# Block 1 of a long convolution goes forward by tokens modulo 4, and GpSimd multiplies gate by up where both lie in SBUF as bf16

## The chip, the cores and the metric

The kernel runs on one core of one Trainium2 chip. The metric is the device time of one execution in microseconds (us), the median of three runs: 909.69 us before the change (909.67 to 910.05). The profile is one more execution, recorded by the hardware profiler. Its engines are TensorE (PE; PEld is its weight load), VectorE (DVE), ScalarE (ACT), GpSimd (POOL) and SyncE (SP, which only issues DMAs).

## The reference, cut to what matters

Four layers follow each other: gated convolution (A), feed-forward (B), A, B, each on a layernorm of x and added to x. S is 2048 tokens, D 576 channels, F 4608.

```python
def A(q, k, v, shift_k, ssm_k, ssm_D):
    k_shift = sum over t of k_pad[:, t:t+S, :] * shift_k[:, ks-1-t]      # four taps
    kv = k_shift * v
    y = causal convolution of kv with ssm_k along the tokens (by FFT), as bf16
    return q * (y + kv * ssm_D)
def B(x, w_gate, w_up, w_down):
    return (gelu(x @ w_gate) * (x @ w_up)) @ w_down
x = x + A(layernorm(x)); x = x + B(layernorm(x)); x = x + A(layernorm(x)); x = x + B(layernorm(x))
```

The convolution's k, v and filter are the same in both A layers, so y is computed once and used twice.

## The kernel before, in words

**Feed-forward.** The tokens are cut into four chunks of 512. A unit is one chunk in one B layer; there are eight units. A unit's 36 tiles of F (128 wide) are done in three parts of 12, and the program goes through 24 *visits* (0 to 23), each one part of one unit. Visits 0 to 2 are unit 0 (chunk 0, first B layer), visits 3, 5 and 7 unit 1 (chunk 1), visits 4, 6 and 8 unit 2, visits 9, 11 and 13 unit 3, visits 10, 12 and 14 unit 4, and so on. For each tile, `gu` (L1103) makes gate and up side by side in one of three PSUM banks that go round; then the tile goes one of two ways (L1689 to L1704). Either ScalarE makes gelu(gate) as fp32 and VectorE multiplies it by up straight from PSUM (L1700, L1701); or ScalarE writes both gelu(gate) and up into SBUF as bf16 (L1691, L1692), so that the bank is free without VectorE, and VectorE multiplies the two there (L1693). The second way is taken while convolution work waits for VectorE. The pair in SBUF is a tile `ga` out of a ring of two; the products are `hT`. After twelve tiles the down part (`two_rows`, L1752, matmuls at L1768) multiplies hT by w_down for the four rows of 128 tokens; a tile's product may be needed from the first matmuls of the down part on.

**Convolution.** It is done by transforms of 512 tokens per block, four blocks. Block 0 is done in a prologue ahead of visit 0. Blocks 1 to 3 are worked off beside the feed-forward matmuls: VectorE makes kv (`kv_ops`, L255 to L267); TensorE transforms the filter's block and kv's block forward in 16 steps; ScalarE evicts each step's result from PSUM to an fp32 tile `eo` (two of its own ring, two of the ring `yh`); VectorE adds and subtracts the halves of eo (`cross`, L333); VectorE multiplies the spectra and sums them (`prod`, L341 to L345, L552), combines them (L353, L358) and folds them (L587, L588); TensorE transforms back (L373 in block 1, L310 in blocks 2 and 3) and ScalarE or VectorE writes y (L697, L700). y of block c is needed before the units of chunk c.

**Forward steps.** For block 1 (`fwd`, `fwd_h`, `fwd_eo`, L469, L497, L295) a step takes one half of the frequencies modulo 2, sums over all four token residues i = 0 to 3 and needs 8 matmuls of 64x288; eo holds the even and the odd tokens' sums, and one `cross` of two VectorE instructions (128x288) finishes two spectra. For blocks 2 and 3 (`fwd4`, `quarter`, L620, L321) a step takes only two token residues (e and e+2) and needs 4 matmuls; a first `cross` makes sums and differences in fp32 tiles `ab` and `cd` (ring `ac`), and for every second step four more VectorE instructions (L656) combine them.

```python
295     def fwd_eo(self, src, kt, s, h, ring, scale=1.0):
...
299                                    [([self.fw(kt, s, i + e) for e in range(2)],
300                                      [src(i + e)[:, h * HW:(h + 1) * HW] for e in range(2)]) for i in (0, 2)])
...
321     def quarter(self, src, e, s, h, scale=1.0):
...
325         ps = yield from self.both_steps(lambda ps: [ps[:, n, 0:HW] for n in range(2)],
326                                    [([self.fw(0, s, i) for i in ij], [src(i)[:, h * HW:(h + 1) * HW] for i in ij])])
```

**What sets the order.** While the program is built, a planner keeps a clock for each engine (`Pace`, L46: `t.pe`, `t.dve`, `t.act`) from cost constants (L29 to L43) and decides where each convolution instruction is put among the feed-forward's. VectorE's convolution work is the list `V`, its adds after forward steps the list `U`, TensorE's steps the list `Pq`, GpSimd's loads the list `L`; `fill` (L1168) drains them after each tile and in the down part. On the chip every engine goes through its instructions in the order so fixed, and waits on semaphores. GpSimd before the change issues DMAs (spectra out to and back from DRAM, L377, L443, L448, L457; k, v, x; outputs L381) and works on statistics of one element per partition (L933, L948, L949). Statistics are put into its order up to AHEAD = 2.0 us before the planner expects their input (L935, L951).

Of the kernel before, what the change touches and what calls it, by code (L numbers as in the profile page):

```python
# [17 lines left out]
P = 128  # L18
# [17 lines left out]
C_HB = 0.345  # L36
C_FOLD = 0.46
C_TURN, DRAIN = 0.0, 0.35
LAG = 0.25
AHEAD = 2.0  # L40
# [5 lines left out]
class Pace:  # L46


    def __init__(self):
        self.pe = self.dve = self.act = 0.0  # L50
# [84 lines left out]
class Conv:  # L135
# [159 lines left out]
    def fwd_eo(self, src, kt, s, h, ring, scale=1.0):  # L295

        nc = self.nc
        ps = yield from self.both_steps(lambda ps: [ps[:, e, 0:HW] for e in range(2)],
                                   [([self.fw(kt, s, i + e) for e in range(2)],
                                     [src(i + e)[:, h * HW:(h + 1) * HW] for e in range(2)]) for i in (0, 2)])  # L300
        eo = self.eo_tile(ring)
        nc.scalar.activation(out=eo[:], in_=ps[:, :, 0:HW], func=ACT.Copy, scale=scale)
        return eo

# [89 lines left out]
    def step(self, m, kv=None, loaded=False):  # L394
# [74 lines left out]
        def fwd(kt, s, h):  # L469
            def run():  # L470
                if s == 0 and h == 0:
                    for k in (kt, kt + 2):
                        kc[k] = self.kcp.tile([P, 2, D], BF16, tag="kc", name="kc")
                free, ring = self.eo_free(True)
                self.eo_at[ring].popleft()
                cur = self.cur
                eo = yield from self.fwd_eo(lambda i: self.vt_[m][:, i, :], kt, s, h, ring)
                done = t.on_act(C_EVA, max(t.pe + 0.25 + LAG, free))
                self.ps_free[cur] = done
                if (kt, s, h) == (1, 1, 1):  # L480
                    self.fwd_at[m] = t.pe + 0.25
                cols = slice(h * HW, (h + 1) * HW)

                def fin():
                    self.cross(eo, kc[kt][:, s, cols], kc[kt + 2][:, s, cols])
                    when = t.on_dve(2 * C_BF, done + LAG)
                    self.eo_at[ring].append(when + LAG)
                    mark(("kc", kt, s, h), when + LAG)
                    if s == 1 and h == 1 and m < self.NB - 1:
                        for k in (kt, kt + 2):  # L490
                            self.spill(self.Kd[m][k], kc[k], when + LAG)
                self.U.append((done + LAG, 2 * C_BF, fin))
            return run

        hh = self.hh if m == 1 else {}

        def fwd_h(kt, s, h):  # L497
            def run():
                if (kt, s, h) == (0, 0, 0):
                    self.hh_tiles()  # L500
                free, ring = self.eo_free(True)
                self.eo_at[ring].popleft()
                cur = self.cur
                eo = yield from self.fwd_eo(self.ht[m], kt, s, h, ring, 1.0 / NFQ)
                done = t.on_act(C_EVA, max(t.pe + 0.25 + LAG, free))
                self.ps_free[cur] = done
                if (kt, s, h) == (1, 1, 1):
                    self.hf_at[m] = t.pe + 0.25
                    if loaded:
                        self.hr_free[0] = self.hr_free[1] = self.hf_at[m]  # L510
                cols = slice(h * HW, (h + 1) * HW)

                def fin():
                    self.cross(eo, hh[kt][:, s, cols], hh[kt + 2][:, s, cols])
                    when = t.on_dve(2 * C_BF, done + LAG)
                    self.eo_at[ring].append(when + LAG)
                    mark(("hh", kt, s, h), when + LAG)
                    if s == 1 and h == 1:
                        for k in (kt, kt + 2):
                            self.spill(self.Hd[m][k], hh[k], when + LAG)  # L520
                        if kt == 1:
                            self.hd_at[m] = when + 10.0
                self.U.append((done + LAG, 2 * C_BF, fin))
            return run
# [95 lines left out]
        def fwd4(filt, e, s, h):  # L620
# [3 lines left out]
            def run():  # L624
                free = self.eo_at["eo"].popleft()
                cur = self.cur
                eo = yield from self.quarter(src, e, s, h, scale)
                done = t.on_act(C_EVA, max(t.pe + 0.13 + LAG, free))
                self.ps_free[cur] = done
                if last:  # L630
                    (self.hf_at if filt else self.fwd_at)[m] = t.pe + 0.13
                cols = slice(h * HW, (h + 1) * HW)

                def first():
# [4 lines left out]
                    else:  # L639
                        if s == 0 and h == 0:  # L640
# [4 lines left out]
                    self.eo_at["eo"].append(t.on_dve(2 * C_BF, done + LAG) + LAG)  # L645

                def second(n):
                    def run():
# [9 lines left out]
                        if n == 1 and last:  # L658
# [7 lines left out]
                            if filt:  # L666
                                self.hd_at[m] = when + 10.0
                    return run
# [40 lines left out]
    def run_loads(self):  # L709
        t = self.t  # L710
        self.flush(t.pe)
        while self.L and self.L[0][0]() <= t.pe - 0.3:
            self.L.popleft()[1]()

# [73 lines left out]
def ssm_geglu_kernel(ctx, tc, A_q, A_k, A_v, A_shift_k, A_ssm_k, A_ssm_D, B_x, B_w_gate, B_w_up,  # L788
# [137 lines left out]
    def mean_after(v, when):  # L926
# [8 lines left out]
        conv.spills.append((when - AHEAD, run))  # L935

    def square_task(get_x, v):
        def run():
# [12 lines left out]
            conv.spills.append((when - AHEAD, root))  # L951
# [255 lines left out]
    with tc.manual_schedule():  # L1207
# [432 lines left out]
        for at, (wb, ph, ui, first, final) in enumerate(visits):  # L1640
# [34 lines left out]
            for fi in range(FP):  # L1675
# [13 lines left out]
                if (hurry() or conv.V and not aq) and t.act <= t.pe + 0.2:  # L1689
# [3 lines left out]
                    nc.vector.tensor_tensor(out=hT[:, fi, :], in0=ga[:, 0, :], in1=ga[:, 1, :], op=ALU.mult)  # L1693
                    there = t.on_act(2 * C_GELU, max(t.pe + 0.15, gone[0]))
                    gone.append(t.on_dve(C_HB, there + 0.15) + 0.1)
# [174 lines left out]
```

## Time and profile before

| what | value |
|---|---|
| median of three runs (range) | 909.69 us (909.67 to 910.05) |
| profiled execution: span from first to last instruction | 907.9 us |
| PE busy | 902.9 us (99%) |
| DVE busy | 556.8 us (61%) |
| ACT busy | 364.5 us (40%) |
| POOL busy | 142.0 us (16%) |
| first gate/up tile of visit 0 | at 44.7 us of the span |
| down part of visit 0 begins | 66.4 us |
| visit 1 begins | 83.05 us |
| visit 2 begins | 118.1 us |
| visit 3 begins | 157.1 us |

The profiled execution's span is what the recorder saw; the runs' time is 1.8 us longer, which lies around the span. A row of a group of instructions reads: line, engine, operation, output tile <- input tiles, partitions x elements, count | busy us, mean ns of one | idle time of the engine ahead of them and what ended it. A row of stages reads: stretch in us from the span's start, its length, then for each engine the busy us and the number of instructions. A row of a source line reads: count, shortest/median/longest in ns. A row of the timeline reads: start, length, instruction, count of merged ones. Matmul records overlap, since matmuls are pipelined, so a matmul's price is taken from a stretch and its count, not from its own duration.

### The profile page before, as it was taken

How to read it: one execution, taken by the hardware profiler on the slowest of the kernel's cores; microseconds unless marked ns; L12 is line 12 of the kernel's file. 1: busy time of each engine (PE TensorE's matmuls, PEld its weight loads, DVE VectorE, ACT ScalarE, POOL GpSimd, SP SyncE). 2: the span in 40 equal slices, each digit the busy share in tenths (PEclk: the TensorE clock that was granted, in tenths of full speed). 3: DMA queues.
4: the chain of work that ended last, by engine and by line, in shares of the span. 5: the costliest groups of instructions: out<-in, count | busy, mean ns of one | idle time of the engine just before them, and what ended most of it. 6: DMA issues, size and time to landing. Idle time of an engine off the chain costs nothing.

```text
span 907.9 us, 24267 instructions
## 1 busy us (share of the span) xinstructions
PE 902.9 (99%) x10465; PEld 601.3 (66%) x10465; DVE 556.8 (61%) x1109; ACT 364.5 (40%) x677; POOL 142.0 (16%) x311
## 2 busy tenths in 40 slices
PE   9999999999999999999999999999999999999998
PEld 7757656577576675775766766757757657667666
DVE  8898988654789876667888744553333334433332
ACT  7784446625434356354244233451121224321211
POOL 5423003320113012230023001220000002100000
PEclk9999999999999999999999999999999999999999
DMA  9999967877519503974934702762720820777630
GB/s 242 314 265 285 231 143 137 179 232 135 170 56 258 128 3 67 270 201 102 251 120 123 167 14 69 138 124 63 136 79 3 157 80 14 142 178 179 135 102 28
DMA packets 128272, 129.73 MB, mean 143 GB/s; under 512 B 43298, under 2 KB 120483, under 8 KB 128164
## 3 DMA queue, kind: packets, MB, share of 16 engines
q1 hardware_dynamic: 119138, 93.22, 47.7%
q0 software_dynamic: 8880, 34.36, 11.0%
q8 instruction: 82, 1.34, 0.6%
q10 hardware_dynamic: 146, 0.59, 0.2%
q14 instruction: 26, 0.21, 0.1%
HBM read 106.91 MB, written 11.80 MB: 131 GB/s over the span
## 4 chain that ended last, share of the span: by engine, by line
PE 98%; POOL 0%; ACT 0%; issue 0%; DVE 0%; ACTq 0%
PE gu L1103 61%; PE dn L1768 30%; PE cps L310 2%; PE ps L284 2%; PE dn L1729 1%; PE ps L1344 0%; PE ps L1103 0%; PE ps L1479 0%; POOL rstd L1564 0%; PE ps L1257 0%; PE ps L1315 0%; PE cps L373 0%; PE ps L278 0%; ACT yh L1526 0%; PE ps L1373 0%
## 5 line engine op out<-in xcount | busy, mean ns | idle before, releaser
L1103 PE MATMUL gu<-xnT,wgu 64*128 64x512 bf16 x5148 | 561.4, 376 | 0.0
L1103 PEld LDWEIGHTS <-wgu 64*128 64x128 bf16 x5220 | 293.2, 94 | 260.6 <-issue 0.7
L1768 PE MATMUL dn<-wd,hT 64*128 64x288 bf16 x4512 | 293.9, 283 | 0.0
L1768 PEld LDWEIGHTS <-hT 64*128 64x128 bf16 x4512 | 254.4, 94 | 26.2
L1700 ACT ACTIVATE ga<-gu 128x512 f32<-128x512 f32 x175 | 104.4, 597 | 311.0 <-PE gu L1103 307.8
L1701 DVE TENSOR_TENSOR hT<-ga,gu 128x512 bf16<-128x512 f32 x175 | 120.1, 687 | 167.5 <-ACT ga L1700 167.3
L1691 ACT ACTIVATE ga<-gu 128x512 bf16<-128x512 f32 x111 | 66.2, 597 | 149.9 <-PE gu L1103 143.9
L1693 DVE TENSOR_TENSOR hT<-ga 128x512 bf16<-128x512 bf16 x112 | 47.0, 421 | 59.6 <-ACT ga L1692 59.5
L1692 ACT CAST ga<-gu 128x512 bf16<-128x512 f32 x111 | 64.3, 579 | 0.0
L933 POOL TENSOR_SCALAR means<-s 128x1 f32<-128x1 f32 x28 | 10.4, 372 | 248.7 <-DVE x_c L1798 219.4
L1804 DVE SCALAR_TENSOR_TENSOR x_c<-dn,means,x_c 128x576 f32<-128x576 f32 x28 | 22.8, 815 | 28.4 <-PE dn L1768 28.4
L1806 DVE TENSOR_TENSOR x_c<-x_c,dn 128x576 f32<-128x576 f32 x32 | 24.1, 752 | 25.8 <-PE dn L1768 25.5
L949 POOL TENSOR_TENSOR rstd<-ve,neghalf_t 128x1 f32<-128x1 f32 x56 | 35.4, 632 | 4.7
L345 DVE TENSOR_TENSOR prod<-prod 128x576 bf16<-128x576 bf16 x64 | 29.3, 458 | 2.2
L328 ACT ACTIVATE eo<-cps 128x576 f32<-128x576 f32 x32 | 20.8, 651 | 23.5 <-PE cps L310 17.3
L1785 DVE TENSOR_TENSOR xn<-x_c,dn 128x576 bf16<-128x576 f32 x15 | 11.3, 754 | 26.5 <-PE dn L1768 24.2
L656 DVE TENSOR_TENSOR kc<-ab,cd 128x288 bf16<-128x288 f32 x64 | 25.3, 452 | 0.0
L443 POOL DMA_DIRECT2D kr<-Kd x20 | 11.2, 558 | 88.2 <-DVE prod L344 88.2
L941 ACT ACTIVATE junk<-x_c,nm 128x576 bf16<-128x576 f32 x28 | 21.5, 769 | 2.2 <-POOL nm L933 1.6
L977 ACT ACTIVATE yh<-y,rstd 128x576 f32<-128x576 bf16 x28 | 21.4, 768 | 1.1 <-POOL rstd L949 1.1
L448 POOL DMA_DIRECT2D hr<-Hd x32 | 17.8, 556 | 24.1 <-DVE prod L344 22.6
L948 POOL TENSOR_SCALAR ve<-ss 128x1 f32<-128x1 f32 x56 | 13.9, 248 | 43.7 <-ACT junk L941 43.4
(177 smaller groups left out, 626.4 us busy)
## 6 DMA issues: line engine op xcount, KB each, us to landing
wgu<-in_B_w_gate_dram SPq DMA_DIRECT2D x45, 576.0 KB, 5.9
wd<-in_B_w_down_dram SPq DMA_DIRECT2D x30, 864.0 KB, 7.1
wgu<-in_B_w_up_dram SPq DMA_DIRECT2D x45, 512.0 KB, 7.5
hr<-Hd POOLq DMA_DIRECT2D x32, 288.0 KB, 4.6
kr<-Kd POOLq DMA_DIRECT2D x24, 288.0 KB, 3.9
Kd<-kc POOLq DMA_DIRECT2D x12, 288.0 KB, 6.4
k<-in_A_k_dram POOLq DMA_DIRECT2D x3, 1008.0 KB, 10.3
wgu<-in_B_w_up_dram SPq DMA_DIRECT2D x45, 64.0 KB, 7.3
```

Source lines behind the costliest of these rows:

```text
L345: nc.vector.tensor_tensor(out=dst[:, cols], in0=pr[:, 0, cols], in1=pr[:, 1, cols], op=ALU.subtract if part == 0 else ALU.add)
L656: nc.vector.tensor_tensor(out=into[k][:, plane, cols], in0=a, in1=b, op=op)
L949: nc.gpsimd.tensor_tensor(out=v["rstd"][:], in0=ve[:], in1=neghalf_t[:, 0:1], op=ALU.pow)
L1103: nc.tensor.matmul(cols(pair[:, s, :]), lhsT=w[r0:r0 + HK, k, gi * P:(gi + 1) * P], rhs=cols(xnT[r0:r0 + HK, blk_of[k], :]), start=(k == 0 ...
L1691: nc.scalar.activation(out=ga[:, 0, :], in_=pair[:, 0, :], func=ACT.Gelu_apprx_tanh)
L1692: nc.scalar.copy(out=ga[:, 1, :], in_=pair[:, 1, :])
L1693: nc.vector.tensor_tensor(out=hT[:, fi, :], in0=ga[:, 0, :], in1=ga[:, 1, :], op=ALU.mult)
L1700: nc.scalar.activation(out=ga[:], in_=pair[:, 0, :], func=ACT.Gelu_apprx_tanh)
L1701: nc.vector.tensor_tensor(out=hT[:, fi, :], in0=ga[:], in1=pair[:, 1, :], op=ALU.mult)
L1768: nc.tensor.matmul(acc[:, g, 0:HW], lhsT=lhs[r], rhs=wn[r, g * HW:(g + 1) * HW], start=step == 0 and fi == 0, stop=step == 1 and fi == FP - 1)
L1804: nc.vector.scalar_tensor_tensor(out=xh, in0=acc[:, :, 0:HW], scalar=m_[:, 0:1], in1=xh, op0=op, op1=ALU.add)
L1806: nc.vector.tensor_tensor(out=xh, in0=xh, in1=acc[:, :, 0:HW], op=ALU.add)
```

## The change

Two things change, and the planner with them.

1. **Block 1 goes forward as blocks 2 and 3 do.** `fwd_eo`, `fwd` and `fwd_h` are gone; block 1 uses `fwd4` and `quarter`, with the eo tiles from both rings as before. Its 16 forward steps have 4 matmuls each, where they had 8, and VectorE has 64 instructions after them (16 ab, 16 cd, 32 combining), where it had 32. All spectra of a transform are finished after its eighth step, and the four are spilled together, where two were finished after the fourth.
2. **GpSimd multiplies gate by up** in the second way of a tile (both in SBUF as bf16), except for the last two tiles of a visit, and when the planner's clock of GpSimd says that it will be free within one tile's time; otherwise VectorE does it.
3. **The planner** has a clock for GpSimd (`t.pool`), to which multiplies, spills and loads are added, and puts statistics into GpSimd's order 1.0 us ahead of their input (NEARLY) in place of 2.0 (AHEAD).

In the built program GpSimd has 81 of the 108 such multiplies, by visits 9, 9, 8, 1, 10, 9, 1, 10, 1, 1, 10, 10, 2 (visits 0 to 12), and VectorE 27; before VectorE had all 112. 180 tiles go the first way, 176 before. TensorE's list has 64 matmuls fewer. Eight of block 1's 16 forward steps stand in visit 0's gate/up part and eight in its down part (six and ten before); block 1's backward steps stand behind tile 6 of visit 2 and later (behind tile 5 before), and block 3's in visit 12's down part (visit 13's before).

```diff
-AHEAD = 2.0
+C_HP, C_Q, C_PS = 1.3, 0.57, 0.4
+NEARLY = 1.0
...
+    def on_pool(self, cost, ready=0.0):
+        self.pool = max(self.pool, ready, self.pe - 1.0) + cost
+        return self.pool
...
-    def quarter(self, src, e, s, h, scale=1.0):
+    def quarter(self, src, e, s, h, ring, scale=1.0):
...
-        eo = self.eop.tile([P, 2, HW], F32, tag="eo", name="eo")
+        eo = self.eo_tile(ring)
...
         while len(self.spills) > keep and self.spills[0][0] <= now:
-            self.spills.popleft()[1]()
+            ready, run = self.spills.popleft()
+            run()
+            self.t.on_pool(C_Q, ready)
...
-                free = self.eo_at["eo"].popleft()
+                free, ring = self.eo_free(m == 1)
+                self.eo_at[ring].popleft()
...
         def steps(filt, ready):
-            limit = lambda: max(ready(), 0.0 if self.eo_at["eo"] else NEVER)
-            if m > 1:
-                for h in range(2):
-                    for e in range(2):
-                        for s in range(2):
-                            self.Pq.append((limit, 0.25, fwd4(filt, e, s, h)))
-                return
-            for kt in range(2):
-                for s in range(2):
-                    for h in range(2):
-                        self.Pq.append((lambda: max(
-                            ready(), 0.0 if self.eo_at["eo"] or self.eo_at["yh"] else NEVER), 0.49, (fwd_h if filt else fwd)(kt, s, h)))
+            limit = lambda: max(ready(), 0.0 if self.eo_at["eo"] or m == 1 and self.eo_at["yh"] else NEVER)
+            for h in range(2):
+                for e in range(2):
+                    for s in range(2):
+                        self.Pq.append((limit, 0.25, fwd4(filt, e, s, h)))
...
-        conv.spills.append((when - AHEAD, run))
+        conv.spills.append((when - NEARLY, run))
...
-                    nc.vector.tensor_tensor(out=hT[:, fi, :], in0=ga[:, 0, :], in1=ga[:, 1, :], op=ALU.mult)
                     there = t.on_act(2 * C_GELU, max(t.pe + 0.15, gone[0]))
-                    gone.append(t.on_dve(C_HB, there + 0.15) + 0.1)
+                    aside = fi < FP - 2 and max(t.pool, there) < t.pe + C_GU
+                    (nc.gpsimd if aside else nc.vector).tensor_tensor(
+                        out=hT[:, fi, :], in0=ga[:, 0, :], in1=ga[:, 1, :], op=ALU.mult)
+                    gone.append((t.on_pool(C_HP, there + 0.2) if aside else t.on_dve(C_HB, there + 0.15)) + 0.1)
```

More of the change, by code (lines that the diff above doesn't have):

```diff
@@ L293, in eo_free @@
         return min((self.eo_at[ring][0], ring) for ring in (("eo", "yh") if wide else ("eo",)) if self.eo_at[ring])
[L295 to L303, printed above, removed]
     def half_rows(self, outs, terms, step):
@@ L467, in step @@
                            load(kt, a)))
[L469 to L493, printed above, removed]
@@ L495, in step @@
-        hh = self.hh if m == 1 else {}
[L497 to L524, printed above, removed]
@@ L631, in run @@
                     (self.hf_at if filt else self.fwd_at)[m] = t.pe + 0.13
+                    if filt and loaded:
+                        self.hr_free[0] = self.hr_free[1] = self.hf_at[m]
                 cols = slice(h * HW, (h + 1) * HW)
@@ L639, in first @@
                     else:
-                        if s == 0 and h == 0:
+                        if s == 0 and h == 0 and filt and m == 1:
+                            self.hh_tiles()
+                        elif s == 0 and h == 0:
                             for k in range(RT):
@@ L667, in run @@
                                 self.hd_at[m] = when + 10.0
+                                for k in range(2):
+                                    for q in range(4):
+                                        mark(("hh", k, q // 2, q % 2), when + LAG)
                     return run
@@ L713, in run_loads @@
             self.L.popleft()[1]()
+            t.on_pool(C_Q)
     def run_v(self, limit):
```

8 lines of the change are left out of this document (4 added, 4 removed).

## Prediction

> **What bounds the kernel now.** I read the page first: busy time, clock and the chain that ended last.
>
> ```profile
> span 907.9 us, 24267 instructions
> PE 902.9 (99%) x10465; PEld 601.3 (66%) x10465; DVE 556.8 (61%) x1109; ACT 364.5 (40%) x677; POOL 142.0 (16%) x311
> ...
> PEclk9999999999999999999999999999999999999999
> ...
> PE 98%; POOL 0%; ACT 0%; issue 0%; DVE 0%; ACTq 0%
> ```
>
> TensorE is busy for 902.9 of 907.9 us at full clock, and 98% of the chain is its own work. So time falls only by TensorE work that goes, at most by the 5.0 us beside it, and rises by whatever makes TensorE wait. A busy figure alone can hide waits inside, so I took stages, one pure down part (the fourth row) and the three stretches from visit 0 to the end of block 1's folds:
>
> ```profile
> core 0: us, PE busy (x) PEld busy (x) DVE busy (x) ACT busy (x) POOL busy (x), PEclk, DMA share, GB/s
> 44.70:83.05 38.35, 38.35 (x492) 26.48 (x489) 35.16 (x74) 26.66 (x54) 10.78 (x22) 1.00 1.04 261
> 83.05:118.10 35.05, 35.05 (x412) 23.05 (x409) 31.57 (x65) 12.88 (x24) 3.22 (x6) 1.00 1.01 252
> 118.10:128.30 10.20, 10.20 (x100) 5.37 (x97) 7.66 (x18) 4.54 (x9) 0.00 (x0) 1.00 0.36 106
> 787.54:799.30 11.76, 11.76 (x194) 10.90 (x192) 2.95 (x4) 0.60 (x1) 1.36 (x3) 1.00 1.03 190
> ```
>
> The down part has 192 matmuls of 64x288 (192 weight loads; two more matmuls straddle its edges) in 11.76 us: 61.25 ns each, back to back. VectorE is the engine next to its limit: from 44.70 to 128.30 it is busy for 35.16 + 31.57 + 7.66 = 74.39 of 83.60 us and idle for 9.21. What it does there has a deadline:
>
> ```profile
> 127.80 0.46 DVE L588 TENSOR_TENSOR yb<-yb 128x576 bf16<-128x576 bf16 x1
> 128.17 0.75 DVE L255 TENSOR_TENSOR kvt<-k,skc 128x1152 bf16<-128x1152 bf16 x1
> 128.84 0.42 DVE L1693 TENSOR_TENSOR hT<-ga 128x512 bf16<-128x512 bf16 x1
> 129.18 0.75 DVE L255 TENSOR_TENSOR kvt<-k,skc 128x1152 bf16<-128x1152 bf16 x1
> ...
> 129.89 0.42 PE L373 MATMUL cps<-w,V 128*128 128x288 bf16 x2
> ```
>
> Block 1's last fold ends at 128.26, and 1.6 us later TensorE, in its fixed order, multiplies by it. If VectorE is late by more than that, all of TensorE stands still.
>
> **Part 1, TensorE.** Block 1's forward matmuls in the trace:
>
> ```profile
> L310 PE MATMUL cps<-v,T 64*128 64x288 bf16 x48 | 6.0, 283 | 0.0
> L310 PE MATMUL cps<-ht,T 64*128 64x288 bf16 x48 | 5.0, 282 | 0.0
> L310 PE MATMUL cps<-v,nT 64*128 64x288 bf16 x16 | 2.8, 283 | 0.0
> L310 PE MATMUL cps<-ht,nT 64*128 64x288 bf16 x16 | 2.4, 282 | 0.0
> ```
>
> 128 in all; half go. 64 x 61.25 ns = **3.92 us** off the path, since nothing else is as long.
>
> **Part 1, VectorE.** 32 more instructions of 128x288, and 24 multiplies moved out of this stage (9 + 9 + 6, by the changed program's order ahead of the folds):
>
> ```profile
> L1693 DVE TENSOR_TENSOR hT<-ga 128x512 bf16<-128x512 bf16 x26 | 10.9, 420 | 6.4 <-ACT ga L1692 6.3
> L333 DVE TENSOR_TENSOR hh<-eo 128x288 bf16<-128x288 f32 x16 | 6.4, 451 | 0.2 <-ACT eo L302 0.2
> L344 DVE TENSOR_TENSOR prod<-kr,hh 128x576 bf16<-128x576 bf16 x8 | 3.3, 451 | 0.0
> L341 DVE TENSOR_TENSOR prod<-kr,hh 128x1152 bf16<-128x1152 bf16 x4 | 3.0, 752 | 0.0
> ```
>
> The crosses take 6.4 / 16 = 0.40 us each, so +12.8. A multiply's slot, from the timeline above, is 129.18 - 128.84 = 0.34 us, so -8.2. VectorE has 4.6 us more to do, in a stage that TensorE leaves 3.9 us sooner; of the 9.2 us of idle time 0.7 is left. Uncontested, the two parts just balance, and the 3.92 us would be kept.
>
> The spills of four spectra together, and the first products, which now need all eight filter steps rather than four, I cost at nothing: in this stage VectorE has the shift products of kv to do meanwhile (L255 and L261). If that cover were gone, the first products' wait is late next.
>
> **Part 2, GpSimd's multiply.** The trace has no wide two-input operation on GpSimd. Its nearest rows:
>
> ```profile
> L948 POOL TENSOR_SCALAR ve<-ss x56: 182/192/598, 65.0 to 780.4; 128x1 f32<-128x1 f32 x56
> L1249 POOL TENSOR_SCALAR_AFFINE_SELECT ident<-ident x1: 293/293/293, 1.8 to 1.8; 128x128 bf16<-128x128 bf16 x1
> L1249 POOL TENSOR_SCALAR_AFFINE_SELECT below<-below x1: 1881/1881/1881, 2.1 to 2.1; 128x128 bf16<-128x128 bf16 x1
> ```
>
> One element takes 192 ns and 128 elements 293: 0.80 ns an element. If two operands come one after the other it is 1.6 ns, so 512 elements take 0.81 us of reading, 1.0 us in all (an estimate). Against it stands a tile's time: 18 matmuls of L1103 (two sides of nine), at 561.4 / 5148 us each by its row below, are 1.96 us. So the multiply by itself is hidden. But the third row above is the same instruction as the second and took 1881 ns. Beside it stood:
>
> ```profile
> L1103 PE MATMUL gu<-xnT,wgu 64*128 64x512 bf16 x5148 | 561.4, 376 | 0.0
> ...
> 2.09 1.88 POOL L1249 TENSOR_SCALAR_AFFINE_SELECT below<-below 128x128 bf16<-128x128 bf16 x1
> ...
> 2.15 0.48 DVE L1277 SCALAR_TENSOR_TENSOR jT<-colT,rowT,offs 128x256 int32<-128x256 f32 x1
> ...
> 2.55 1.27 DVE L1277 SCALAR_TENSOR_TENSOR jT<-colT,rowT,offs 128x256 int32<-128x256 f32 x3
> ...
> 63.11 0.62 POOL L933 TENSOR_SCALAR means<-s 128x1 f32<-128x1 f32 x1 [2.19 <-ACT junk L922]
> ...
> 62.91 0.75 DVE L341 TENSOR_TENSOR prod<-kr,hh 128x1152 bf16<-128x1152 bf16 x1
> ```
>
> VectorE's four instructions with two SBUF inputs end at 3.82 us; GpSimd ends 0.15 us later. At 63 us the one-element operation ends 0.07 us after VectorE's product. So the two engines share a way into SBUF, and GpSimd waited. What a long GpSimd read does to VectorE no row shows, and I bound it: at least nothing, at most the whole 0.81 us of reading. Nearly all of VectorE's work in this stage reads two tiles of SBUF.
>
> [...]
>
> [...]
>
> Sum for block 1, with the way as one shared resource: 24 x 0.81 = 19.4 us more against 0.7 us of room, so 18.7 us too much. Part of it fits where VectorE does not read: 576 further elements cost 752 - 451 = 0.30 us, so 1152 take 0.60, while
>
> ```profile
> 316.70 1.42 DVE L255 TENSOR_TENSOR kvt<-k,skc 128x1152 bf16<-128x1152 bf16 x2
> ...
> 315.98 0.46 DVE L588 TENSOR_TENSOR yb<-yb 128x576 bf16<-128x576 bf16 x1
> ...
> 323.58 0.30 PE L310 MATMUL cps<-w,V 64*128 64x288 bf16 x2
> ...
> 505.02:526.91 21.89, 21.89 (x288) 16.20 (x286) 19.12 (x41) 5.09 (x10) 0.00 (x0) 1.00 0.54 137
> ```
>
> has the second start 1.42 - 0.75 = 0.67 us after the first: 0.07 us free in each, 11 us in the stage's 157 instructions. So the loss lies between 18.7 - 11 = 7.7 and 18.7; I take the middle, **13.2 us**, as neither end has a nearer row. Where it shows: first in visit 0, where a late cross keeps an eo tile, so ScalarE's next eviction and TensorE's next forward step; then at the folds.
>
> Blocks 2 and 3: block 2's folds end at 316.44 and are needed at 323.58, 7.1 us later, so its 20 multiplies (20 x (0.81 - 0.34) = 9.4) cost little. Block 3 moves a visit ahead, so most of the 19.12 us of VectorE work in the last row must come before 505; between 0 and 8 us are lost, and I take 2, since block 2's room is nearest.
>
> **What queues behind.** A multiply waits for ScalarE's copy, and behind it in GpSimd's order stand loads, spills and statistics. ScalarE needs the multiply's `ga` back two tiles later, and TensorE the bank that ScalarE then frees. The statistics' smaller lead is hidden: GpSimd mostly waits.
>
> Sum on the profiled execution: 907.9 - 3.9 + 13.2 + 2 = 919.2 us of span; with the 1.8 us that the median lies above it, **921.0 us**.
>
> **Rivals.**
> - *The gain is kept* (the other side, faster). GpSimd's reads fit between VectorE's and delay nothing. For it: 0.07 us free per instruction and a one-element read that cost VectorE nothing; against it: 1881 ns. It gives 909.7 - 3.9 = 905.8, and 906.5 if some waits come back. It decides below 3.92 / 24 = 0.16 us lost for each multiply.
> - *It cancels*: 0.16 us per multiply or near, 908 to 911.5.
> - *GpSimd is starved or stuck in its own order*, and TensorE waits for hT or `ga`. The affine row's 1.59 us of waiting on each of the 24 multiplies is 38 us, which no tile's time covers fully; also
>
> ```profile
> POOL kr L443 <- DVE prod L344: 88.2, 11, 30.3
> ```
>
>  a load that waits for a late product now holds multiplies behind it; such waits cost nothing before, as nothing urgent followed. It gives 909.7 - 3.9 + 25 to 45, about 940.
> - That too few multiplies move is settled: 81 of 108 do.
>
> **How the numbers follow.** Forecast (912 to 931) 0.48; gain kept 0.25; cancels 0.07; starved 0.20. A measurement tells about 0.2% (1.8 us) from no change, so faster is 0.25, same 0.07, slower 0.68. The likeliest case's own range is 912 to 931. The range over cases is 905 to 935: it takes in the kept gain and leaves out most of the starved case.
>
> **What would show it.** Matmuls L310 at 16 fewer per four steps (right whatever the time). GpSimd's multiplies near 1.0 us where VectorE is idle (visit 4) and longer in visits 0 to 2; VectorE idle or stretched while GpSimd reads; TensorE gaps ahead of forward steps in visit 0 and ahead of L373's successor in visit 2, 13 us together. Wrong if these gaps are absent, or if they stand ahead of gate/up matmuls, waiting for ScalarE and `ga`, at tens of us.

## The result, and the profile after

The changed kernel takes **965.98 us** (median of four runs, 965.07 to 966.46) against 909.7 us: a ratio of **1.0616** (95% interval 1.0601 to 1.0631), 56.3 us slower. The forecast was 921.0 us with a range of 905 to 935: the sign was right, and the time lies far above the range. Times here and below are medians of executions that agree with each other; one of run 14, at 1354 us with a granted clock of 0.66, is left out.

The page of the kernel after, the lines that answer to those of before:

```profile
span 964.3 us, 24183 instructions
PE 920.3 (95%) x10401; PEld 552.3 (57%) x10401; DVE 610.5 (63%) x1061; ACT 361.9 (38%) x672; POOL 244.7 (25%) x392
...
PEclk9998988999989999999898999999999999999999
...
PE 75%; DVE 20%; issue 2%; ACT 1%; POOL 1%; DMA 1%; ACTq 0%; DVEq 0%; POOLq 0%
```

TensorE has 64 matmuls fewer (10465 to 10401), as foretold, but 20% of the chain is now VectorE's. Two numbers add up to the loss: TensorE's time beside its work (span less busy) rises from 907.9 - 902.9 = 5.0 us to 964.3 - 920.3 = 44.0 us (+39.0), and its busy time rises by 17.4 us although it has less to do. VectorE runs 48 instructions fewer and is busy for 53.7 us longer.

The stages of after, in the columns of the stage rows above (stretch, its length, then PE, PEld, DVE, ACT, POOL busy). The second is a visit's gate/up part, the others are down parts:

```profile
114.93:135.93 21.00, 14.20 (x194) 10.27 (x192) 18.13 (x36) 1.07 (x2) 1.64 (x3) 0.84 0.81 213
216.75:240.05 23.30, 23.30 (x220) 12.26 (x216) 2.58 (x4) 11.81 (x22) 12.83 (x13) 1.00 0.55 104
277.56:295.75 18.19, 15.07 (x194) 10.63 (x192) 15.79 (x28) 1.07 (x2) 3.70 (x6) 0.81 0.23 68
470.45:490.91 20.46, 14.49 (x194) 10.33 (x192) 18.71 (x31) 1.07 (x2) 3.42 (x5) 0.83 0.66 158
514.22:538.05 23.83, 15.17 (x196) 10.20 (x194) 21.13 (x34) 2.15 (x4) 5.45 (x8) 0.79 0.28 87
```

A down part that took 11.76 us before takes 18 to 24 us, in block 1 (the first row), block 2 (277) and block 3 (470, 514). In each, VectorE is busy for 86 to 91% of the stretch and the granted clock is 0.79 to 0.84. In visit 4 (the second row), where ten multiplies run on GpSimd and VectorE works for only 2.58 us, nothing is lost.

What TensorE waits for there, from the list of waits of after (engine, line <- releaser: us in total, times, longest; the first two rows are the same stops, seen by the weight load and by the matmul), and the two rows of the multiply's line (count, shortest/median/longest in ns):

```profile
PEld L1714 <- DVE hT L1639: 27.0, 11, 7.7
PE dn L1714 <- DVE hT L1639: 24.0, 5, 7.3
ACT ga L1635 <- POOL hT L1639: 16.7, 13, 4.2
...
POOL kr L440 <- DVE prod L339: 26.0, 6, 12.8
```

```profile
L1639 POOL TENSOR_TENSOR hT<-ga x81: 1146/1167/1752, 45.5 to 559.9; 128x512 bf16<-128x512 bf16 x81
L1639 DVE TENSOR_TENSOR hT<-ga x27: 417/419/426, 74.0 to 563.3; 128x512 bf16<-128x512 bf16 x27
```

The down matmuls wait for multiplies on **VectorE**, the 27 that stayed there (tiles 10 and 11 of a visit), not for GpSimd's. The timeline of after in visit 11's down part shows why:

```profile
513.51 0.59 POOL L440 DMA_DIRECT2D kr<-Kd  x1 [4.22 <-DVE prod L339]
...
514.41 2.83 DVE L340 TENSOR_TENSOR prod<-prod 128x576 bf16<-128x576 bf16 x1
514.66 2.27 POOL L1639 TENSOR_TENSOR hT<-ga 128x512 bf16<-128x512 bf16 x2
...
517.28 0.76 DVE L494 TENSOR_TENSOR ac<-prod 128x576 f32<-128x576 bf16 x1
...
525.25 0.75 DVE L1639 TENSOR_TENSOR hT<-ga 128x512 bf16<-128x512 bf16 x2
525.72 0.10 PEld L1714 LDWEIGHTS <-hT 64*128 64x128 bf16 x2 [7.65 <-DVE hT L1639]
525.72 2.67 PE L1714 MATMUL dn<-wd,hT 64*128 64x288 bf16 x20 [7.34 <-DVE hT L1639]
```

An addition that takes 0.46 us elsewhere takes 2.83 us: it lies beside two GpSimd multiplies, which end at 516.93, and ends 0.31 us later. VectorE then works without a gap through eight more us of products and additions that its order puts ahead of the two multiplies at 525.25, and TensorE has stood for 7.34 us. GpSimd's own multiplies are late too: ahead of them a load waited for 4.22 us for a late product of VectorE.

The same source line over the whole run, first before, then after:

```profile
L345 DVE TENSOR_TENSOR prod<-prod x64: 457/458/460, 78.4 to 515.0; 128x576 bf16<-128x576 bf16 x64
```

```profile
L340 DVE TENSOR_TENSOR prod<-prod x64: 457/458/2835, 104.4 to 556.0; 128x576 bf16<-128x576 bf16 x64
```

The shortest and the median are the same; some instructions are several times as long. I set each VectorE instruction of a trace against the median of its shape before, and call the sum of the differences the **stretch**. In after it is 66.1 us, all of it in the 105 instructions that overlap a GpSimd multiply: 0.82 us for each of the 81 multiplies. All 105 have two inputs in SBUF; no VectorE instruction with an input in PSUM lies beside one. Where one instruction meets one multiply (93 times), nine in ten are at most 0.96 us longer; seven, where the multiply follows within 0.02 us on the issue of a load on GpSimd, are 1.10 to 1.86 us longer.

### The profile page after: what moved, and what is told of

The parts are those of the page before. It is cut to its first block, busy times and chain, and to the rows that moved or that the text cites. A ratio compares the mean times of both kernels' runs of the same rounds, so it can differ in the third digit from the quotient of the medians.

```text
span 964.3 us, 24183 instructions
## 1 busy us (share of the span) xinstructions
PE 920.3 (95%) x10401; PEld 552.3 (57%) x10401; DVE 610.5 (63%) x1061; ACT 361.9 (38%) x672; POOL 244.7 (25%) x392
## 4 chain that ended last, share of the span: by engine, by line
PE 75%; DVE 20%; issue 2%; ACT 1%; POOL 1%; DMA 1%; ACTq 0%; DVEq 0%; POOLq 0%
PE gu L1047 42%; PE dn L1714 27%; DVE prod L339 3%; DVE ac L494 3%; DVE prod L336 2%; DVE prod L340 2%; DVE kvt L260 2%; PE cps L305 1%; PE ps L289 1%; DVE yb L348 1%; DVE kvt L266 1%; DVE cd L328 1%; DVE yb L530 1%; DVE kc L603 1%; DVE yb L353 1%
## 5 line engine op out<-in xcount | busy, mean ns | idle before, releaser
L1047 PEld LDWEIGHTS <-wgu 64*128 64x128 bf16 x5220 | 268.0, 94 | 291.9 <-issue 7.8
L1714 PE MATMUL dn<-wd,hT 64*128 64x288 bf16 x4512 | 308.6, 291 | 29.9 <-DVE hT L1639 24.0
L1714 PEld LDWEIGHTS <-hT 64*128 64x128 bf16 x4512 | 234.0, 97 | 92.5 <-DVE hT L1639 27.0
L1639 POOL TENSOR_TENSOR hT<-ga 128x512 bf16<-128x512 bf16 x81 | 102.1, 1265 | 163.8 <-ACT ga L1636 163.6
L323 ACT ACTIVATE eo<-cps 128x576 f32<-128x576 f32 x48 | 31.0, 653 | 32.2 <-PE cps L305 22.9
L603 DVE TENSOR_TENSOR kc<-ab,cd 128x288 bf16<-128x288 f32 x80 | 34.4, 487 | 0.0
L1639 DVE TENSOR_TENSOR hT<-ga 128x512 bf16<-128x512 bf16 x27 | 10.7, 420 | 26.3 <-ACT ga L1636 26.3
L1731 DVE TENSOR_TENSOR xn<-x_c,dn 128x576 bf16<-128x576 f32 x15 | 11.3, 754 | 24.5 <-PE dn L1714 22.2
L494 DVE TENSOR_TENSOR ac<-ac,prod 128x576 f32<-128x576 f32 x24 | 25.7, 1070 | 0.7
L328 DVE TENSOR_TENSOR ab<-eo 128x288 f32<-128x288 f32 x48 | 20.4, 472 | 8.6 <-ACT eo L323 6.3
L328 DVE TENSOR_TENSOR cd<-eo 128x288 f32<-128x288 f32 x48 | 22.7, 514 | 3.5 <-ACT eo L323 2.8
```

The costliest lines, as they stand in the source:

```text
L328: self.nc.vector.tensor_tensor(out=dst, in0=eo[:, 0, :], in1=eo[:, 1, :], op=op)
L494: nc.vector.tensor_tensor(out=into, in0=prs[part, 0, kt] if a == 1 else into, in1=prs[part, a, kt], op=ALU.add)
L603: nc.vector.tensor_tensor(out=into[k][:, plane, cols], in0=a, in1=b, op=op)
L1047: nc.tensor.matmul(cols(pair[:, s, :]), lhsT=w[r0:r0 + HK, k, gi * P:(gi + 1) * P], rhs=cols(xnT[r0:r0 + HK, blk_of[k], :]), start=(k == 0 ...
L1639: (nc.gpsimd if aside else nc.vector).tensor_tensor(out=hT[:, fi, :], in0=ga[:, 0, :], in1=ga[:, 1, :], op=ALU.mult)
L1714: nc.tensor.matmul(acc[:, g, 0:HW], lhsT=lhs[r], rhs=wn[r, g * HW:(g + 1) * HW], start=step == 0 and fi == 0, stop=step == 1 and fi == FP - 1)
```

## The experiments

Theory **T1**: while a GpSimd instruction reads SBUF, a VectorE instruction with two SBUF inputs stands; VectorE falls behind, and its lateness comes out as stops of TensorE. Rivals: **T2**, GpSimd's own pace and order (1.17 us per multiply, loads queued ahead) is what delays hT; **T3**, block 1's 32 further VectorE instructions are the main cost, and later visits only hand it on.

**1. The same order, every multiply on VectorE.**

```
-                    (nc.gpsimd if aside else nc.vector).tensor_tensor(
+                    nc.vector.tensor_tensor(
```

> The changed kernel with every instruction in the same order, but all 108 bf16 multiplies on VectorE. Theory 1 (a GpSimd instruction that reads two operands keeps VectorE's two-input instructions waiting; their durations above the medians of before sum to 66 us in the changed kernel): VectorE gets 81 x 0.34 = 28 us of work back and loses the 66 us of waiting, so 38 us of the 56 lost come back: 920 to 935 us, and no VectorE group is longer than before. Theory 2 (GpSimd's own pace of 1.27 us a multiply and its queue make hT and ga late): under 912 us, as VectorE's multiply takes 0.42 us. Theory 3 (block 1's 32 further VectorE instructions make VectorE late): 960 us or more.

Measured: 928.3 us (922.8 to 931.0), ratio 1.0196 (1.0156 to 1.0236), stretch 0.2 us. So some 37 of the 56 us (35 to 43 by the execution) come from where the multiply runs. The rest is not contention; runs 11 and 12 take it apart.

**2. GpSimd reads one operand** (it copies gelu(gate); the multiplication by up is left out for the 81 tiles).

```
+                    if aside:
+                        nc.gpsimd.tensor_copy(out=hT[:, fi, :], in_=ga[:, 0, :])
+                    else:
...
```

> GpSimd copies one operand (gelu of gate) where it multiplied two; the multiplication by up is left out for 81 tiles. Theory 1: half the reading, so half of the 66 us by which VectorE's instructions were longer, 30 to 36 us, and 0.4 to 0.5 us longer for one that meets it in place of up to 0.96: 920 to 940 us. Theory 2: GpSimd's instruction is about half as long, VectorE's durations are as before: 910 to 925 us. Theory 3: 960 us or more.

Measured: 917.7 us, ratio 1.0087 (1.0065 to 1.011). The copy's row:

```profile
L1640 POOL COPY hT<-ga x81: 609/705/1281, 45.0 to 508.7; 128x512 bf16<-128x512 bf16 x81
```

The stretch is 24.5 us, at most 0.41 us in nine of ten meetings: smaller than T1 had it, and the time is 2 us under its range and inside T2's. What speaks against T2 here is the stretch alone: T2 said that VectorE would not change, and it did.

**3. GpSimd only writes** (one column is multiplied, hT is then filled with zeros twice, so GpSimd is as busy; the product is left out for the 81 tiles).

```
+                    if aside:
+                        nc.gpsimd.tensor_tensor(out=hT[:, fi, 0:1], in0=ga[:, 0, 0:1], in1=ga[:, 1, 0:1], op=ALU.mult)
+                        for _ in range(2):
+                            nc.gpsimd.memset(hT[:, fi, 1:CH], 0.0)
```

> GpSimd multiplies one column of two operands and then fills hT twice with zeros, so that it is busy about as long but reads one element a partition; the product is left out for 81 tiles. Theory 1: VectorE's durations are as before (sum above the medians under 3 us), and it is rid of 81 multiplies: 905 to 909 us. Theory 2: GpSimd's time and order are as in the changed kernel, so 950 to 970 us. Theory 3: 955 to 966 us.

Measured: 915.1 us (909.6 to 916.3), ratio 1.004 (1.0022 to 1.0059). GpSimd's groups (busy us, mean ns):

```profile
L1642 POOL MEMSET hT<- 128x511 bf16 x162 | 84.5, 521 | 4.7
...
L1640 POOL TENSOR_TENSOR hT<-ga 128x1 bf16<-128x1 bf16 x81 | 27.3, 337 | 145.2 <-ACT ga L1636 144.7
```

GpSimd spends (84.5 + 27.3) / 81 = 1.38 us on each tile, more than in after, in the same order and behind the same loads, and the stretch is 0.25 us. **T2 falls**: GpSimd's pace and queue alone do not cost 50 us. The 6 us above T1's range had another cause (run 11).

**4. GpSimd's multiply without part 1** (the second part of the change put on the kernel before; 75 multiplies go to GpSimd).

> Part 2 alone: the kernel before with GpSimd's multiplies (75 of them) and the planner's clock for GpSimd; block 1 goes forward in 16 steps of 8 matmuls as before. Theory 1: 75/81 of 66 us, so 55 to 62 us longer VectorE instructions: 945 to 965 us. Theory 2: the same, 945 to 965 us, but with VectorE's durations unchanged. Theory 3: 907 to 912 us.

Measured: 954.6 us, ratio 1.0493 (1.0472 to 1.0514), stretch 58.3 us, or 0.78 us per multiply. T3 falls: without the new transform the loss is 45 of the 56 us. T1 and T2 gave the same time; the stretch speaks for T1.

**5. Part 1 without GpSimd.**

```
-C_HB = 0.345
+C_HB = 0.36
...
-NEARLY = 1.0
+NEARLY = 2.0
...
-                    aside = fi < FP - 2 and max(t.pool, there) < t.pe + C_GU
+                    aside = False
```

> Part 1 alone: block 1 by tokens modulo 4, every multiply on VectorE both in the plan and on the chip, the old lead of the statistics (2.0), and 0.36 in place of 0.345 us as the planner's cost of a multiply (the plan does not close with 0.345). The planner then knows of all the work on VectorE. T1 and T3 agree here that block 1 pays for 32 more crosses (12.8 us) against 9.2 us of idle VectorE time and 3.9 us less TensorE work: 909.7 - 3.9 + 12.8 - 5.3 of idle time that is left within the shorter stage = about 913, range 909 to 920, VectorE's instructions unchanged (under 1 us longer in all). If the transform by itself were the main cost of the change (T3), it would give 925 or more. If it were the gain that the 3.92 us suggest, 906.

Measured: 921.9 us, ratio 1.0136 (1.0121 to 1.0151): above T1's range and below T3's 925, 12.2 us lost. Stages of this kernel:

```profile
118.00:153.20 35.20, 35.20 (x402) 22.54 (x399) 28.94 (x63) 15.84 (x30) 2.56 (x6) 1.00 0.81 182
153.20:160.00 6.80, 1.94 (x24) 1.48 (x22) 4.67 (x14) 6.55 (x13) 3.98 (x11) 0.91 0.37 124
160.00:165.00 5.00, 2.81 (x25) 2.27 (x23) 2.19 (x4) 0.30 (x2) 1.32 (x3) 0.50 0.39 118
165.00:170.00 5.00, 4.15 (x26) 1.88 (x26) 0.76 (x1) 0.30 (x1) 0.00 (x0) 0.60 0.02 3
```

Until 153.2 TensorE loses almost nothing. Then gate/up work has run out: visit 3 needs block 1's output, whose folds VectorE finishes too late, and from 153.2 to 170 TensorE works for 8.90 of 16.8 us, part of it at half clock. The planner also puts 36 small transposes on TensorE there, from 157.7 to 164.8, that the kernel before has not. So here work that VectorE does late in a block is paid for at the hand-over to the next block, not where it is added.

**6. Tiles 10 and 11 on GpSimd too.**

```
-                    aside = fi < FP - 2 and max(t.pool, there) < t.pe + C_GU
+                    aside = max(t.pool, there) < t.pe + C_GU
```

> As after, but tiles 10 and 11 of a visit may go to GpSimd too. T1 with the place that the trace shows (down parts stand because the multiplies of tiles 10 and 11 wait in VectorE's order behind late convolution work): the stops ahead of the down parts, some 49 us in visits 0, 1, 5, 7, 10 and 11, mostly go, though GpSimd's own multiply is 0.8 us slower and VectorE's lateness then comes out at the folds: 930 to 950. Rival (VectorE's lateness sets the end wherever it shows, the last two tiles only make it visible): 955 to 975, with the waits on hT replaced by waits on the products and folds. VectorE's instructions longer by 0.8 us for each multiply on GpSimd in both.

Measured: 973.9 us, ratio 1.0705 (1.0689 to 1.0721). The rival holds: the two last tiles only make the lateness visible.

```profile
PE dn L1714 <- POOL hT L1639: 13.2, 8, 4.2
PE dn L1714 <- DVE x_c L1752: 8.3, 3, 4.0
PE dn L1714 <- DVE hT L1639: 7.3, 1, 7.3
PE cps L305 <- DVEq L1079: 3.8, 2, 3.4
```

The waits on VectorE's hT fall from 24.0 to 7.3 us, and others take their place. 102 multiplies stretch VectorE by 83.6 us, again 0.82 us each.

**7 and 8. GpSimd in the early visits only, and in the late ones only.**

```
-                    (nc.gpsimd if aside else nc.vector).tensor_tensor(
+                    (nc.gpsimd if aside and at <= 2 else nc.vector).tensor_tensor(
```

> After's order of instructions, with GpSimd taking the multiply in visits 0 to 2 only (26 of 81), VectorE the rest. T1, with each stage paying for its own contested multiplies: the order alone costs 928.3, and visits 0 to 2 lost 23.4 us in after against 13.1 us with all multiplies on VectorE, so 928.3 + 10.3 = 938, range 932 to 944; VectorE's instructions some 21 us longer in all. T3 (block 1's stage is where the change costs, the later visits only hand it on): 950 or more.

> After's order of instructions, with GpSimd taking the multiply from visit 5 on only (43 of 81), VectorE the rest. T1, additive: visits 5 to 11 lost 32.2 us in after against 7.1 us with all multiplies on VectorE, so 928.3 + 25.1 = 953, range 945 to 960; VectorE's instructions some 37 us longer in all. T3: block 1 keeps its multiplies on VectorE, so 928 to 938.

Measured: 939.8 us, ratio 1.0333 (1.0317 to 1.0348), stretch 23.4 us, for the early visits; 950.8 us, ratio 1.0431 (1.04 to 1.0462), stretch 41.3 us, for the late ones. Each set pays for its own multiplies, and the late ones pay more. T3 falls here too. (From visit 5 on there are 44 multiplies, not 43: 26 + 11 + 44 = 81.)

**9. The same reads in two instructions each** (81 multiplies as 162 of 256 columns).

```
+                    for q in range(2 if aside else 1):
+                        r = slice(q * CH // 2, (q + 1) * CH // 2) if aside else slice(0, CH)
```

> As after, but each of GpSimd's 81 multiplies is issued as two of 256 columns. T1, if VectorE waits as long as GpSimd reads, whatever the size of the instruction: the longest wait in one meeting falls from 0.96 to about 0.5 us, the sum stays near 66 us longer instructions (60 to 75, as 0.2 us of fixed cost is added per multiply), and the time stays at 958 to 975. Rival: VectorE loses one whole GpSimd instruction per meeting and can slip in between two, so that shorter ones halve the loss: 30 to 40 us longer and 930 to 948.

Measured: 959.2 us, ratio 1.0544 (1.0527 to 1.056).

```profile
L1641 POOL TENSOR_TENSOR hT<-ga x162: 657/872/1232, 45.5 to 553.6; 128x256 bf16<-128x256 bf16 x162
```

The stretch is 62.9 us, in T1's range, and where a VectorE instruction meets one half, nine in ten are at most 0.47 us longer. What counts is how long GpSimd reads, not in how many instructions (62.9 us for 162 halves, 66.1 for 81 whole ones).

**10. Only half of block 1's transform modulo 4, multiplies on VectorE**: the filter alone, and kv alone.

> The kernel before with only block 1's filter, not kv, transformed by tokens modulo 4, and every multiply on VectorE: TensorE 1.96 us less, VectorE 16 crosses of 0.40 us = 6.4 us more, in a stage with 9.2 us of idle time. T3 by proportion to part 1 alone (12.2 + 3.9 = 16.1 us lost for 12.8 us of work): 909.7 - 2 + 8 = 916. If VectorE's idle time takes it in, 907.7; range 907 to 917.

> The kernel before with only block 1's kv, not the filter, transformed by tokens modulo 4: TensorE 1.96 us less, VectorE 6.4 us more, later in the stage than with the filter alone (911.5). If VectorE's idle time of 9.2 us takes in the first 6.4 us whichever half it is: 909 to 912. If the later half has the less room (all of it falls ahead of the folds): 913 to 918.

Measured: 911.5 us, ratio 1.0021 (1.0012 to 1.003), and 911.6 us, ratio 1.0017 (1.0008 to 1.0025). Each half loses 1.8 us, both together 12.2 (run 5). The pages, the filter alone first:

```profile
PE 903.0 (99%) x10451; PEld 601.3 (66%) x10451; DVE 563.1 (62%) x1128; ACT 365.2 (40%) x678; POOL 146.1 (16%) x311
PE 903.5 (99%) x10460; PEld 598.8 (66%) x10460; DVE 565.0 (62%) x1130; ACT 365.4 (40%) x678; POOL 140.4 (15%) x311
```

TensorE's time beside its work is 6.4 and 6.3 us, where it was 5.0: VectorE's room takes in the first 6.4 us of added crosses almost whole, whichever half they are, and not the second 6.4. But TensorE's busy time does not fall either. 32 matmuls went, and the planner put 18 and 27 of the small transposes there (from 149 to 156 us) that the kernel before has not. Neither version beats the kernel before.

**11 and 12. Two loads of spectra later on GpSimd's queue**: behind the four spills and the next statistics, with all other orders as they were; on the write-only kernel of run 3 (the product left out again) and on the kernel of run 1.

```
+    def later(self, hold, tile, src):
+        put = lambda: self.nc.gpsimd.dma_start(out=tile[:].rearrange("p s d -> p (s d)"), in_=src)
+        self.held.append((self.t.pe + 9.0, put)) if hold else put()
```

> GpSimd only writes hT (the product of gate and up is left out for the 81 tiles), as in the earlier run that gave 915.1, but two loads of spectra on GpSimd's queue, issued there at 64.6 us, stand behind the four spills and the statistics of the next tile as in the kernel before (70.3 us). If those early loads are what made transfers between 62 and 74 us take 18 to 24 us and held the gate weights of visit 1 back by 4.3 us: the stop at 82 us goes, and with nothing reading SBUF on GpSimd part 1's 3.92 us show: 904.5 to 908. If not (something else slows the transfers): 909 to 916 as before, with landings still 18 to 24 us after the issue.

> After's order with every multiply on VectorE, and the same two loads issued later. If the early loads slow the transfers: some 4 to 6 us less than 928.3, 920 to 925; what remains above 909.7 is VectorE's load in block 1 (part 1 alone gave 921.9). If not: 923 to 931.

Measured: 909.7 us (908.5 to 913.5), ratio 1.0006 (0.9996 to 1.0015), and 923.0 us (922.0 to 924.3), ratio 1.0146 (1.0132 to 1.016). The transfers issued from 60 to 76 us of the span, first in run 3, then with the loads late (count, KB each, median us from issue to landing):

```profile
Hd<-hh POOLq DMA_DIRECT2D x4, 288.0 KB, 18.3
wgu<-in_B_w_gate_dram SPq DMA_DIRECT2D x1, 576.0 KB, 17.9
...
nat<-in_A_ssm_k_dram SPq DMA_TRANSPOSE x1, 24.4
```

```profile
Hd<-hh POOLq DMA_DIRECT2D x4, 288.0 KB, 5.8
wgu<-in_B_w_gate_dram SPq DMA_DIRECT2D x1, 576.0 KB, 9.2
...
nat<-in_A_ssm_k_dram SPq DMA_TRANSPOSE x1, 14.5
```

They land in 32 to 59% of the time, and run 3's stop of 4.3 us at the start of visit 1 is gone. Only the two loads were moved, so the early loads cause the slow landings and the stop; both expectations hold in that. How they stop TensorE is not shown. The list of waits of run 3 has:

```profile
PE gu L1047 <- issue: 4.3, 1, 4.3
```

The stop comes behind the fifth matmul of visit 1, and "issue" means that TensorE waited for nothing that the profile shows. The gate weights that landed late, at 91.3 us, are first used at 102.5; those of visit 1's first tiles had landed by 67. So it is not these weights that were held back, as the expectation has it.

The gain that the first expectation promised, 904.5 to 908, does not come: with nothing read on GpSimd the change ends level with the kernel before. In its profile (an execution of 911.7 us) the gate/up matmuls of visit 3 come 2.1 us sooner than in before, so part of the gain is there; later a stop of 2.1 us for `x_c`, at 440.5 us, and 3.4 us at half clock behind it take it back.

**13. GpSimd in the half-idle visits 3 and 4 only**, on the base of 923.0 us.

```
+                    (nc.gpsimd if aside and at in (3, 4) else nc.vector).tensor_tensor(
```

> The order with every multiply on VectorE and the two loads late (923.0), with GpSimd taking the multiply in visits 3 and 4 only (11 of 81), where VectorE is busy for half of the time (11.81 of 23.30 us in visit 4). T1 with room: VectorE waits here too (4 to 9 us longer in all), but has idle time for it, so 922.5 to 925. Rival (each multiply costs the same wherever it lies, 26 + 43 of them 39.3 us, 0.57 each): 923 + 6.3 = 929.

(The 11.81 us in it is ScalarE's column; VectorE's is 2.58.) Measured: 924.7 us, ratio 1.0153 (1.0134 to 1.0172), which the intervals do not part from 923.0.

```profile
L1646 POOL TENSOR_TENSOR hT<-ga x11: 1149/1152/1157, 183.0 to 218.6; 128x512 bf16<-128x512 bf16 x11
```

VectorE is not stretched at all, so the 4 to 9 us were wrong: in these visits it hardly works while GpSimd reads. The row gives the multiply's own length, 1.15 us.

**14. The late visits again, on the base of 923.0 us** (`at >= 5`, 44 multiplies).

> The same base (923.0) with GpSimd taking the multiply from visit 5 on only (43 of 81). The former run of this split stood on the order with early loads, whose times spread over 9 us. T1: 923.0 + 22.5 = 945.5, range 941 to 949, in stops ahead of the down parts of visits 5, 7, 10 and 11; block 2's 20 multiplies alone would then cost some 8 to 10 us, not the nothing that the prediction gave them. If the former figure was the early loads in part: 935 to 941.

Measured: 946.5 us (944.4 to 946.7), ratio 1.0391 (1.037 to 1.0413), stretch 41.5 us: 23.5 us over its base, for 44 multiplies. One stretch of it, in visit 11:

```profile
494.00:505.00 11.00, 2.77 (x34) 1.51 (x32) 10.69 (x19) 2.15 (x4) 3.49 (x6) 0.75 0.43 147
```

VectorE is busy for 10.69 of 11 us, TensorE for 2.77.

**The account.** 909.7 before; +13.3 for the changed order with every multiply on VectorE, transfers undisturbed (923.0): part 1's work on VectorE, and what the planner's new order costs in later visits (3.3 of the 8.7 us of TensorE's stops in run 12's profile lie behind block 1); +16.8 for the 26 multiplies of visits 0 to 2 (939.8; run 7 issued the two loads at 67.7 us, so 923.0 is its base); +1.7 for the 11 of visits 3 and 4; +23.5 for the 44 from visit 5 on. The sum is 965.0, and 966.0 was measured.

## Why the prediction was wrong

- **What bounds the kernel**: right. TensorE bounds it, VectorE is next, and time is lost where VectorE's deadline passes.
- **Part 1, TensorE**: the 64 matmuls went, as the page's count shows. The 3.92 us never showed in the time: even with free multiplies the kernel is level with the one before (run 11).
- **Part 1, VectorE, "the two parts just balance, and the 3.92 us would be kept"**: too good. The prediction's own terms with the multiplies left on VectorE give 12.8 - (9.2 - 3.9) = 7.5 us too much, less 3.9, so +3.6; measured were +13.3, and +12.2 with an order planned for it. The 9.2 us of idle time were counted as room for all of it: 6.4 us of crosses went in (run 10), 12.8 did not (run 5).
- **Spills and first products at nothing**: not refuted in after, where the two loads were issued at 67.7 us. In the same order they were issued at 62 to 65 us in runs 1 and 3, and that cost some 5 us: a cost in the place that I had passed over, from the loads and not from the spills.
- **GpSimd's multiply, 1.0 us**: measured 1.15 with VectorE hardly working beside it (run 13), 1.27 on the average in after. The 0.15 us that the estimate lacked is 24 x 0.15 = 3.6 us in the sum, which would have made 924.6, still far too low.
- **VectorE's wait, 0 to 0.81 us per multiply**: the upper bound, 0.82 on the average. It was my estimate from GpSimd's reading time; no row of before shows VectorE's wait. In after 85 of the 93 meetings go by who began first: VectorE is longer in 44 of the 45 that GpSimd began, and not in 41 of the 48 that VectorE began; the other seven of these 48 are the longest waits, 1.10 to 1.86 us. Beside GpSimd instructions that write and read next to nothing VectorE is stretched by 0.25 us in all (run 3).
- **Block 1, "the loss lies between 7.7 and 18.7"**: the gaps of 0.07 us did not take in 11 us. The 26 multiplies stretched VectorE by 23.4 us and cost 16.8, and with most of run 12's 13.3 block 1 paid up to 30.1 us where the sum had -3.9 + 13.2 = +9.3. The places were partly right: eo in visit 0, and the folds; the stop of 6.80 us in visit 1's down part was not named.
- **Blocks 2 and 3, "I take 2": the step that failed most.** They cost 23.5 us, 21.5 more than the sum had (block 1 came out up to 20.8 over). I read block 2's room from one deadline, its last folds (7.1 us), and took block 3's cost from the nearest of those. The deadline that decides comes sooner and in every visit: in VectorE's order, which is fixed, the multiplies of tiles 10 and 11 stand behind convolution work, so any lateness stops the down part in the same visit. And run 6 shows that without that deadline another takes its place.
- **What queues behind**: GpSimd's loads do hold multiplies back (16.7 us of ScalarE waiting for GpSimd's hT; 7.8 in run 3, where VectorE is not stretched), in good part as a result of VectorE's lateness. What this adds by itself was not separated.
- **The clock was missing from the sum.** The prediction priced a stop at its length. TensorE's busy time rose by 17.4 us with 3.9 us less to do. In seven stretches behind stops, 47.8 us in all, the granted clock of after is 0.50; TensorE is busy for 35.8 us in them, so about 17.9 us of busy time are the clock's (an estimate: half of it). The other 3.4 us were not traced.
- **The rivals**: "the gain is kept" is refuted, "starved or stuck" came nearest in size (940) and had the direction of the wait wrong: in after VectorE's instructions are 0.82 us longer for each multiply, GpSimd's multiply 0.11 us longer than in run 13 (1.265 us on the average against 1.152).

## What to carry to other kernels

Before work is given to GpSimd, count VectorE's instructions with two SBUF inputs beside it: here nine in ten of those that met one multiply of 1.15 us were at most 0.96 us longer, and 0.34 us freed was paid with 0.82 on the average. The idle share of an engine is not room (VectorE's 9.2 us took in 6.4 us of crosses here, not 12.8); room is what is left up to its next deadline in its own order, visit by visit, and the last small instruction that another engine waits for is that deadline. And a stop of TensorE can cost more than its length: behind six of the seven stops of over 2 us in after the granted clock was 0.50 for 3.4 to 10.2 us.

## What was not expected of the hardware

**The wait is GpSimd's reading time.** A one-element operation on GpSimd (`ve`) takes 0.19 us, the median of 56 in before. Nine in ten of the VectorE instructions that met one GpSimd instruction waited at most 0.96 us beside multiplies of 1.15 (after), 0.47 beside halves of 0.66 (run 9), 0.41 beside copies of 0.61 (run 2): each time the instruction's length less about 0.19 us. Beside writes there was no wait: a stretch of 0.25 us over 162 of them (run 3). Who begins first decides: of the 93 meetings in after, GpSimd's multiply began first in 45, and 44 of these VectorE instructions are longer; VectorE began first in 48, and 41 of them are not. The other seven are the longest waits, 1.10 to 1.86 us, each at a multiply right behind the issue of a load; why these wait was not settled.

**The clock after a stop.** Stages of after behind the stop of visit 11 (the clock is the number ahead of the last two):

```profile
520.00:525.72 5.72, 0.00 (x0) 0.00 (x0) 5.55 (x12) 0.00 (x0) 1.42 (x3) 0.61 0.53 164
525.72:528.00 2.28, 2.28 (x20) 1.32 (x22) 2.21 (x6) 0.00 (x0) 0.29 (x1) 0.50 0.26 105
528.00:531.00 3.00, 3.00 (x28) 1.87 (x26) 1.57 (x3) 0.00 (x0) 0.25 (x1) 0.50 0.37 98
531.00:536.00 5.00, 5.00 (x82) 3.75 (x78) 4.53 (x8) 0.00 (x0) 0.00 (x0) 0.95 0.01 3
```

After the stop TensorE runs for more than 5 us at half clock: 48 matmuls in 5.28 us, 110 ns each against 61.25. The stretches of half clock in the trace of after are 3.4, 6.8 or 10.2 us long; this one is 10.2 and begins 2.9 us after TensorE has stopped. Not every stop has one: TensorE stood seven times for more than 2 us, and after the first, from 62.43 to 65.36 us, the clock stayed at 1.00 up to 74.16. What decides it was not tried.

**Loads beside a transposing transfer.** Two loads of 288 KB, issued between 62 and 65 us of the span instead of 67 to 80, about doubled the landing times of what was issued around them. In the four profiles with loads at 62 to 65 us (runs 1, 2, 3 and 8) the gate weights issued next, at 70 to 75 us, landed 16 to 19 us later; in before, after and runs 5, 7, 11 and 12 in 7 to 11. Run 4 does not fit the issue time of the loads alone: its loads were issued at 67 to 70 us, yet those weights took 25.9 us; two spills of 288 KB were issued there at 63.4 and 64.0. In all of these the transposing load of the filter was issued at 61 to 63 us; that it has a part in it was not tried.
